# Attention and GELU feed-forward on one core: q and k of a head pair transposed together in four array quadrants, and layer 2 of the first chunk taken by quarters of its weights

## The chip, the cores and the metric

The kernel runs on one core of a Trainium2 chip. The core has five engines that run their own instruction streams and wait for each other by semaphores: TensorE (PE in the profile, with its weight loads as PEld), VectorE (DVE), ScalarE (ACT), GpSimd (POOL) and SyncE (SP). PE writes its results to PSUM, eight banks of which are shared out by hand here; DVE and ACT empty them into SBUF. DMAs are issued from POOL (loads) and SP (stores, and the transposing DMAs described below).

The metric is the device time of one execution in microseconds, as the median of several runs. Times in the profile are from one profiled execution, counted from its first instruction.

## The reference

What is computed, cut to what matters (8 batches, 8 heads, 576 tokens, 64 values per head; 4,608 tokens in all):

```python
scores = scale * q @ k.T                       # per batch and head, scale = 1/8
cum    = cumsum(max(s, 0))                     # over the tokens
bias   = -(cum[i] - cum[j])                    # added as min(bias, 0)
attn   = softmax(where(causal, scores + bias)) # over j
x      = attn @ v                              # as [4608, 512]: heads side by side
h      = x @ w_in                              # [4608, 2048]
g      = 0.5 * h * (1 + erf(h / sqrt(2)))      # exact GELU
out    = g @ w_out                             # [4608, 512]
```

## The kernel before, in words

**Two tilings that run against each other.** Attention goes by batches of 576 tokens, four pairs of heads (`p` = 0 to 3) each. The feed-forward part goes by nine chunks `c` of 512 tokens. In chunk `c` the kernel does layer 1 (`l1_item`, L487) for the 512 tokens, and then layer 2 (`l2_item`, L513) mixed with the attention of batch `c + 1`, whose result `xT` is what layer 1 of the next chunk reads. Layer 2 of a chunk is four blocks of 128 tokens (`sub`), each a sum over 16 slices of `w_out` (`ft`); an `l2_item` does the slices from `f0` to `f1` with two matmuls of 512 columns each (two column halves of the array), and after the last slice a DVE copy to `o_sb` (L530) and a store follow.

**Attention of one batch.** The steps for a pair `p` are: q and k stand transposed in `qkT`; `sc_item` (L370) makes the scores with ten matmuls and two exponentials on ACT (L394), and DVE applies the causal mask (L403, L408); `av_item` (L464) multiplies with v (`num`) and with the weights of the bias (`den`), 16 matmuls, and `norm` (L429) divides: logarithm and exponential on ACT (L433, L434), and a product on DVE (L449) that writes `xT`. v is scaled on DVE first (L230, called by `scale_pair`). The last 64 tokens of a batch are handled by `av_rest` and `norm_rest` for all pairs at once.

**How q and k get transposed.** From batch 2 on they go through DRAM: DVE interleaves two heads (L178), SP writes rows and reads them back with transposing DMAs (L194). Batches 0 and 1 come too early for that and are transposed on PE by `tr_item` (L353). `load_pair` (batch 0, one pair) and `load_early` (batch 1, two pairs) put q into one tile `early_q` and k into another, `early_k`: partitions 0 to 63 hold pairs 0 and 1, partitions 64 to 127 pairs 2 and 3. A partition holds nine consecutive tokens of a head. So one `tr_item` is 18 transposes of 64x64 (nine tokens `r`, two heads `e`) out of one row half of the array, the two heads going to the two column halves; then one copy (L364, DVE, for the very first on ACT) to `qkT`.

**PSUM.** Tag `sc` has two tiles of two banks (scores, layer 1, and `avw`), `av` three tiles of one bank, `mlp` one. The `av` tiles serve the transposes (`tr_ps`), the products with v (`avn`, `avd`), the rest tile `avr`, and those layer 2 sums that are called with `av=True`; other layer 2 sums are in `mlp`. A new tile of a tag takes a bank whose last reader is done, and PE waits for that reader.

**What sets the order.** The scheduling is by hand: each engine runs its instructions in the order in which the program names them. The start (L575 to L623) works through batch 0, with warm-up matmuls (`keep_busy`) between; L625 begins the loop over chunks, and L649 to L695 is the special mix of chunk 0 with batch 1. POOL's loads are issued in program order too, and later ones are held by small copies to `pace` (L643, L692, L721) until some result is there. The four loads of `w_out` (L611, slices 0-3, 4-7, 8-11, 12-15) are issued between the two halves of batch 1's q and k.

Of the kernel before, what the change touches and what calls it, by code (L numbers as in the profile page):

```python
# [19 lines left out]
def kernel(  # L20
# [10 lines left out]
    nc = tc.nc  # L31
    fp32 = mybir.dt.float32
    bf16 = mybir.dt.bfloat16
# [5 lines left out]
    B, H, S, D = q.shape  # L39
# [53 lines left out]
    G = 9  # L93
    early = {}

    def load_early(b, n, p):
        src = q if n == "q" else k
        if p == 0:
            early[b, n] = work.tile([128, 2, 2, G * D], bf16, tag=f"raw{n}", bufs=3, name=f"early_{n}")
        e0 = (p // 2) * 64  # L100
        nc.gpsimd.dma_start(
            out=early[b, n][e0 : e0 + 64].rearrange("g j e f -> g (j e) f"),
            in_=bass.AP(
                tensor=src.tensor,
                offset=src.offset + (b * H + 2 * p) * S * D,
                ap=[[G * D, 64], [S * D, 4], [1, G * D]],
            ),
        )

    def load_pair(b, n, p):  # L110
        src = q if n == "q" else k
        if p == 0:
            early[b, n] = work.tile([128, 2, 2, G * D], bf16, tag=f"raw{n}", bufs=3, name=f"early_{n}")
        e0 = (p // 2) * 64
        nc.gpsimd.dma_start(
            out=early[b, n][e0 : e0 + 64, p % 2],
            in_=bass.AP(
                tensor=src.tensor,
                offset=src.offset + (b * H + 2 * p) * S * D,
                ap=[[G * D, 64], [S * D, 2], [1, G * D]],  # L120
            ),
        )
# [227 lines left out]
        nc.vector.tensor_copy(bad, n)  # L350


    def tr_item(b, p, i, copy=None):  # L353
        t_ps = ps.tile([128, G, 64], bf16, tag="av", bufs=3, name="tr_ps")
        e0 = (p // 2) * 64
        src = early[b, "qk"[i]]
        for r in range(G):
            for e in range(2):
                nc.tensor.transpose(  # L359
                    t_ps[e * 64 : e * 64 + 64, r, :],  # L360
                    src[e0 : e0 + 64, p % 2, e, r * D : (r + 1) * D],
                    ident_bf[e0 : e0 + 64, e0 : e0 + 64],
                )
        (copy or nc.vector.tensor_copy)(  # L364
            qkT[b % 2][:, i, p, :S].rearrange("d (g r) -> d g r", r=G), t_ps.rearrange("d r g -> d g r")
        )

    P_of = {}

# [94 lines left out]
    def av_item(b, p, wide=False, rest=True):  # L464
        num, den = av_banks(wide)
        av_mm(b, p, num, MAIN, False)
        av_mm(b, p, den, MAIN, True)
        if rest:
            av_rest(b, p)
        norm(b, p, p + 1, num, den, 0, CUT, [(0, 0, 256), (1, 256, CUT)])  # L470
# [91 lines left out]
    def scale_pair(b, p):  # L562
        scale_v(b, ((0, ST - 1), (ST - 1, ST)), nc.vector, 2 * p, 2 * p + 2)
# [7 lines left out]
    def keep_busy(n):  # L571
        for _ in range(n):
            nc.tensor.matmul(warm, lhsT=busy[:, :128], rhs=busy, start=True, stop=True)  # L573

    weights_scan()  # L575
    keep_busy(8)
    tr_item(0, 0, 0, nc.scalar.copy)
    keep_busy(1)
    tr_item(0, 0, 1)
    keep_busy(1)  # L580
    tr_item(0, 1, 0)
    keep_busy(1)
    sc_item(0, 0, masks=False)
    nc.vector.tensor_scalar(neg_bf, tri_bf, 2048.0, -2048.0, op0=MULT, op1=ALU.add)
    tr_item(0, 1, 1)
    weights_dve()
    keep_busy(2)
    sc_item(0, 1, neg=True, units=(0,))
    tr_item(0, 2, 0)
    sc_item(0, 1, neg=True, units=(1,))  # L590
    weights_pe()
    tr_item(0, 2, 1)
    mask_item(0, 0, 0, nc.vector)
    tr_item(0, 3, 0)
    sc_item(0, 2, neg=True)
    tr_item(0, 3, 1)
    mask_item(0, 0, 1, nc.vector)
    keep_busy(1)
    sc_item(0, 3, neg=True)
# [25 lines left out]
    for c in range(NCH):  # L625
        nb = c + 1
        for k0, k1 in ((0, 2), (2, 3)) if c == 0 else ((0, 3),):
            l1_item(c, 0, k0, k1)
            l1_item(c, 1, k0, k1)
        l1_item(c, 0, KO - 1)  # L630
        l1_item(c, 1, KO - 1)
        l1_item(c, 2, av=True)
        if 0 < c and nb < B:
            scale_v(nb, STS, nc.vector)
            absmax_v(nb)
        if c == 0:
# [12 lines left out]
        if c == 0:  # L649
            exp_set()  # L650
            load_v(2)
            for p in range(NP):
                av_rest(0, p)
            tr_item(1, 0, 0)
            tr_item(1, 0, 1)
            l2_item(c, 0, 0, 8)
            tr_item(1, 1, 0)
            tr_item(1, 1, 1)
            norm_rest(0)
            sc_item(1, 0)  # L660
            l2_item(c, 1, 0, 8, av=True)
            sc_item(1, 1)
            l2_item(c, 0, 8)
            tr_item(1, 2, 0)
            tr_item(1, 2, 1)
            l2_item(c, 1, 8, av=True)
            tr_item(1, 3, 0)
            tr_item(1, 3, 1)
            scale_pair(1, 0)
            sc_item(1, 2)  # L670
            l2_item(c, 2, 0, 8, av=True)
            scale_pair(1, 1)
            sc_item(1, 3)
            l2_item(c, 2, 8, av=True)
            scale_pair(1, 2)
            av_item(1, 0, rest=False)
            scale_pair(1, 3)
            av_item(1, 1, wide=True, rest=False)
            l2_item(c, 3, 0, 8)
            interleave(2, "q")  # L680
            write_rows(2, 0, nc.sync)
            av_item(1, 2, wide=True, rest=False)
            l2_item(c, 3, 8)
            interleave(2, "k")
            write_rows(2, 1, nc.sync)
            av_item(1, 3, rest=False)
            for p in (0, 1):
                transpose_rows(2, p)
            gelu_set()
            for p in (2, 3):  # L690
                transpose_rows(2, p)
            nc.gpsimd.tensor_copy(pace, qkT[0][:, 1, 3, 0:1])  # L692
            load_qk(3)
            load_v(3)
            absmax_v(1)  # L695
        elif nb < B:
# [196 lines left out]
```

## Time and profile before

| What | Value |
|---|---|
| median of 14 runs | 331.6 us |
| lowest and highest run | 328.98 and 336.56 us |
| the profiled execution: device time | 334.04 us |
| its span, first to last instruction | 332.3 us |
| PE busy | 319.7 us, 96% |
| ACT busy | 202.2 us, 61% |
| DVE busy | 194.0 us, 58% |
| DMA, mean over the span | 143 GB/s |
| transposes on PE (`tr_ps`), share of the chain | 1% |
| layer 1 and layer 2, share of the chain | 36% and 35% |

How to read it: a line of the chain in order of time gives the start, the length and the engine with the tile, the source line and the number of instructions. A timeline line gives start, length, engine, line, operation, `out<-in`, shapes, count, and in square brackets how long the engine stood idle before it and what ended that. In the profile the names have no buffer numbers: `o_ps` is any layer 2 sum.

### The profile page before, as it was taken

How to read it: one execution, taken by the hardware profiler on the slowest of the kernel's cores; microseconds unless marked ns; L12 is line 12 of the kernel's file. 1: busy time of each engine (PE TensorE's matmuls, PEld its weight loads, DVE VectorE, ACT ScalarE, POOL GpSimd, SP SyncE). 2: the span in 40 equal slices, each digit the busy share in tenths (PEclk: the TensorE clock that was granted, in tenths of full speed). 3: DMA queues.
4: the chain of work that ended last, by engine and by line, in shares of the span. 5: the costliest groups of instructions: out<-in, count | busy, mean ns of one | idle time of the engine just before them, and what ended most of it. 6: DMA issues, size and time to landing. Idle time of an engine off the chain costs nothing.

```text
span 332.3 us, 8737 instructions
## 1 busy us (share of the span) xinstructions
PE 319.7 (96%) x3754; PEld 193.9 (58%) x3754; DVE 194.0 (58%) x385; ACT 202.2 (61%) x287; POOL 65.7 (20%) x100
## 2 busy tenths in 40 slices
PE   8879999999999999997999999999999999999993
PEld 4456666656666556654565566656665666555552
DVE  5659269996569365945477457945693664140021
ACT  3785757769576857675575777586768676204500
POOL 8754243005200740700026001400000000000000
PEclk9998999999999999999899999999999999999999
DMA  8999999845984899999869965725410010010012
GB/s 128 219 211 200 206 190 270 251 91 94 238 250 107 149 253 275 153 158 150 271 130 193 240 193 104 174 77 172 117 51 32 35 64 2 34 63 35 1 65 71
DMA packets 53837, 47.45 MB, mean 143 GB/s; under 512 B 31328, under 2 KB 43872, under 8 KB 53792
## 3 DMA queue, kind: packets, MB, share of 16 engines
q0 software_dynamic: 15936, 23.07, 39.3%
q1 hardware_dynamic: 37856, 23.75, 27.6%
q8 instruction: 31, 0.51, 0.6%
q14 instruction: 14, 0.11, 0.1%
HBM read 36.85 MB, written 16.52 MB: 161 GB/s over the span
## 4 chain that ended last, share of the span: by engine, by line
PE 90%; DMA 5%; ACT 2%; DVE 1%; issue 0%; SPq 0%
PE h_ps L501 36%; PE o_ps L523 35%; PE sc_ps L378 5%; DMA qkT<-rows 5%; PE avn L416 4%; PE avd L416 3%; PE tr_ps L359 1%; PE warm L573 1%; PE avr L416 1%; ACT P L394 1%; PE o_ps L544 1%; DVE qkT L364 1%; PE avw L416 1%; PE sc_ps L386 0%; ACT ln L434 0%; ACT ln L433 0%
## 5 line engine op out<-in xcount | busy, mean ns | idle before, releaser
L523 PE MATMUL o_ps<-w_out_r,gT 128*64 128x512 bf16 x1120 | 131.1, 383 | 0.1
L501 PE MATMUL h_ps<-xT,w_in_r 128*64 128x512 bf16 x1152 | 127.8, 383 | 1.9 <-DVE xT L449 1.9
L501 PEld LDWEIGHTS <-w_in_r 128*64 128x64 bf16 x1152 | 75.8, 111 | 51.9 <-issue 3.8
L523 PEld LDWEIGHTS <-gT 128*64 128x64 bf16 x1120 | 62.5, 111 | 49.8 <-issue 1.6
L508 ACT ACTIVATE gT<-h_ps 128x1024 bf16<-128x1024 f32 x54 | 54.3, 1022 | 50.6 <-PE h_ps L501 50.6
L394 ACT ACTIVATE P<-sc_ps 128x1024 bf16<-128x1024 f32 x64 | 62.1, 1020 | 36.5 <-PE sc_ps L378 34.3
L530 DVE COPY o_sb<-o_ps 128x512 f32<-128x512 f32 x35 | 24.0, 687 | 47.6 <-PE o_ps L523 47.5
L403 DVE TENSOR_TENSOR P<-P,tri_bf 128x512 bf16<-128x512 bf16 x58 | 24.1, 422 | 39.6 <-ACT P L394 39.4
L213 DVE TENSOR_REDUCE amx<-qkT 128x2 f32<-128x1152 bf16 x32 | 40.9, 1335 | 0.0
L202 POOL DMA_DIRECT2D raw_v<-in_v_dram x40 | 34.3, 885 | 10.7 <-DMA w_out_r<-in_moe_w_out_dram 4.2
L449 DVE SCALAR_TENSOR_TENSOR xT<-avn,ln 128x256 bf16<-128x256 f32 (+3 forms) x64 | 21.7, 385 | 24.2 <-ACT ln L434 24.1
L230 DVE TENSOR_TENSOR vv<-raw_v,wb 128x512 bf16<-128x512 f32 (+3 forms) x44 | 25.2, 632 | 0.0
L433 ACT ACTIVATE ln<-avd 128x256 f32<-128x256 f32 x56 | 18.6, 392 | 10.9 <-PE avd L416 10.9
L434 ACT ACTIVATE ln<-ln 128x512 f32<-128x512 f32 (+1 forms) x40 | 23.5, 587 | 1.3
L378 PE MATMUL sc_ps<-qkT 64*128 64x256 bf16 (+2 forms) x320 | 20.9, 250 | 3.3 <-DMA qkT<-rows 1.9
L511 ACT ACTIVATE gT<-h_ps 128x512 bf16<-128x512 f32 x36 | 19.6, 603 | 6.3 <-PE h_ps L501 6.3
L220 DVE TENSOR_REDUCE amv<-raw_v 128x1 f32<-128x2048 f32 (+1 forms) x16 | 22.9, 1470 | 0.0
L378 PEld LDWEIGHTS <-qkT 64*128 64x128 bf16 x320 | 12.9, 94 | 17.1 <-issue 10.3
L416 PEld LDWEIGHTS <-vv 128*64 128x64 bf16 x384 | 18.0, 110 | 4.1
L416 PEld LDWEIGHTS <-wb 128*64 128x64 bf16 x384 | 17.6, 112 | 0.6 <-issue 0.5
L364 DVE COPY qkT<-tr_ps 128x576 bf16<-128x576 bf16 x15 | 10.9, 753 | 10.2 <-PE tr_ps L359 10.2
L416 PE MATMUL avd<-P,wb 128*64 128x256 bf16 x224 | 15.8, 263 | 0.0
(94 smaller groups left out, 165.0 us busy)
## 6 DMA issues: line engine op xcount, KB each, us to landing
out_dram<-o_sb SPq DMA_DIRECT2D x35, 256.0 KB, 3.0
raw_v<-in_v_dram POOLq DMA_DIRECT2D x32, 256.0 KB, 8.7
rows<-qk_bf SPq DMA_DIRECT2D x12, 576.0 KB, 6.3
early_q<-in_q_dram POOLq DMA_DIRECT2D x14, 288.0 KB, 11.2
early_k<-in_k_dram POOLq DMA_DIRECT2D x14, 288.0 KB, 12.3
w_in_r<-in_moe_w_in_dram POOLq DMA_DIRECT2D x4, 512.0 KB, 10.8
w_out_r<-in_moe_w_out_dram POOLq DMA_DIRECT2D x4, 512.0 KB, 15.4
raw_v<-in_v_dram POOLq DMA_DIRECT2D x8, 128.0 KB, 10.2
```

What stands on the lines that cost most here:

```text
L202: nc.gpsimd.dma_start(out=t[:n_st, st, :, :], in_=bass.AP(tensor=v.tensor, offset=v.offset + b * H * S * D + st * 128 * D, ap=[[D, n_st], ...
L213: nc.vector.tensor_reduce(amx[:, b * NP + p], qkT[b % 2][:, :, p, :S], axis=AX, op=ALU.max, apply_absolute_value=True)
L230: eng.tensor_tensor(vb[:n_st, st0:st1, h0:h1, :], t[:n_st, st0:st1, h0:h1, :], wb[:n_st, st0:st1, b * H + h0 : b * H + h1] .unsqueeze(3).t ...
L378: nc.tensor.matmul(s_ps[:, e, off : off + n], lhsT=qkT[b % 2][e * 64 : e * 64 + 64, 1, p, jt * 128 : jt * 128 + 128], rhs=qkT[b % 2][e * 6 ...
L394: nc.scalar.activation(P[:, :, UO[u] : UO[u] + UW[u]], s_ps[:, :, : UW[u]], func=AF.Exp, scale=scale)
L403: eng.tensor_tensor(d, d, tri_bf.unsqueeze(1).unsqueeze(1).to_broadcast([128, 2, 2, 128]), op=MULT)
L416: nc.tensor.matmul(out[e * 64 : e * 64 + 64, lo : lo + n], lhsT=(wb[:, jt, b * H + h : b * H + h + 1].to_broadcast([128, 64]) if den else ...
L434: nc.scalar.activation(ln[:, :w], ln[:, :w], func=AF.Exp, scale=-1.0)
L501: nc.tensor.matmul(h_of[c, f2][i][e * 64 : e * 64 + 64], lhsT=w_in_r[:, ko, ft * 128 + e * 64 : ft * 128 + e * 64 + 64], rhs=xT[:, ko, c * ...
L508: nc.scalar.activation(gT_of[c][:, f2 * 2 : f2 * 2 + 2, :], hh_of[c, f2], func=AF.Gelu)
L523: nc.tensor.matmul(o_ps[e * 64 : e * 64 + 64], lhsT=gT[:, ft, t0 : t0 + 64], rhs=w_out_r[:, ft, :], start=(ft == 0), stop=(ft == FT - 1), ...
L530: nc.vector.tensor_copy(o_sb, o_ps)
```

## The change

It has three parts.

1. **Tiles.** For batches 0 and 1, q and k of a pair now lie in the same tile: q in partitions 0 to 63, k in 64 to 127. There is a tile for pairs 0 and 1 and one for pairs 2 and 3 (tags `rawqk0`, `rawqk1`, three buffers each), besides those of the later batches. The loads and their order stay.
2. **Transposes.** `tr_items` takes q and k of a pair together: in each of nine rounds it issues two transposes of q (upper row half) and two of k (lower row half) into two `av` tiles, and then copies both. In the start it does so for pairs 0 and 1 of batch 0, with the warm-up matmuls put together around them; pairs 2 and 3 of batch 0 are still taken q and k apart. For batch 1 all four pairs are taken together.
3. **Order in chunk 0.** Layer 2 of chunk 0 goes by quarters (four slices, 8 matmuls) for blocks 0, 1 and 3, block 2 moves ahead of the transposes of pairs 2 and 3 and into an `av` tile, and the scores, products and scalings of batch 1 stand at other places between these pieces.

The diff, cut to its core:

```diff
+    def early_tile(b, n, p):
+        key = "qk"[p // 2] if b < 2 else n
+        if (b, key) not in early:
+            early[b, key] = work.tile([128, 2, 2, G * D], bf16, tag=f"raw{key}", bufs=3, name=f"early_{key}")
+        return early[b, key], (int(n == "k") if b < 2 else p // 2) * 64
...
-    def tr_item(b, p, i, copy=None):
-        t_ps = ps.tile([128, G, 64], bf16, tag="av", bufs=3, name="tr_ps")
-        e0 = (p // 2) * 64
-        src = early[b, "qk"[i]]
+    def tr_items(b, p, its, copies=None):
+        src = early[b, "qk"[p // 2]]
+        t_ps = {i: ps.tile([128, G, 64], bf16, tag="av", bufs=3, name="tr_ps") for i in its}
         for r in range(G):
-            for e in range(2):
-                nc.tensor.transpose(
...
+            for i in its:
+                e0 = i * 64
+                for e in range(2):
+                    nc.tensor.transpose(
+                        t_ps[i][e * 64 : e * 64 + 64, r, :],
+                        src[e0 : e0 + 64, p % 2, e, r * D : (r + 1) * D],
+                        ident_bf[e0 : e0 + 64, e0 : e0 + 64],
+                    )
+        for i in its:
+            (copies[i] if copies else nc.vector.tensor_copy)(
+                qkT[b % 2][:, i, p, :S].rearrange("d (g r) -> d g r", r=G),
+                t_ps[i].rearrange("d r g -> d g r"),
+            )
...
     weights_scan()
-    keep_busy(8)
-    tr_item(0, 0, 0, nc.scalar.copy)
-    keep_busy(1)
-    tr_item(0, 0, 1)
-    keep_busy(1)
-    tr_item(0, 1, 0)
-    keep_busy(1)
+    keep_busy(9)
+    tr_items(0, 0, (0, 1), (nc.scalar.copy, nc.vector.tensor_copy))
+    keep_busy(2)
     sc_item(0, 0, masks=False)
     nc.vector.tensor_scalar(neg_bf, tri_bf, 2048.0, -2048.0, op0=MULT, op1=ALU.add)
-    tr_item(0, 1, 1)
+    tr_items(0, 1, (0, 1))
...
             for p in range(NP):
                 av_rest(0, p)
-            tr_item(1, 0, 0)
-            tr_item(1, 0, 1)
-            l2_item(c, 0, 0, 8)
-            tr_item(1, 1, 0)
-            tr_item(1, 1, 1)
+            tr_items(1, 0, (0, 1))
+            l2_item(c, 0, 0, 4)
+            tr_items(1, 1, (0, 1))
             norm_rest(0)
+            l2_item(c, 1, 0, 4, av=True)
             sc_item(1, 0)
-            l2_item(c, 1, 0, 8, av=True)
+            l2_item(c, 0, 4, 8)
+            l2_item(c, 1, 4, 8, av=True)
             sc_item(1, 1)
-            l2_item(c, 0, 8)
-            tr_item(1, 2, 0)
-            tr_item(1, 2, 1)
-            l2_item(c, 1, 8, av=True)
-            tr_item(1, 3, 0)
-            tr_item(1, 3, 1)
+            l2_item(c, 0, 8, 12)
+            l2_item(c, 1, 8, 12, av=True)
+            l2_item(c, 2, 0, 12, av=True)
+            l2_item(c, 0, 12)
+            l2_item(c, 1, 12, av=True)
+            tr_items(1, 2, (0, 1))
+            l2_item(c, 2, 12, av=True)
+            tr_items(1, 3, (0, 1))
             scale_pair(1, 0)
+            l2_item(c, 3, 0, 4)
             sc_item(1, 2)
-            l2_item(c, 2, 0, 8, av=True)
             scale_pair(1, 1)
+            l2_item(c, 3, 4, 8)
             sc_item(1, 3)
-            l2_item(c, 2, 8, av=True)
             scale_pair(1, 2)
             av_item(1, 0, rest=False)
             scale_pair(1, 3)
+            l2_item(c, 3, 8, 12)
             av_item(1, 1, wide=True, rest=False)
-            l2_item(c, 3, 0, 8)
             interleave(2, "q")
             write_rows(2, 0, nc.sync)
             av_item(1, 2, wide=True, rest=False)
-            l2_item(c, 3, 8)
+            l2_item(c, 3, 12)
             interleave(2, "k")
             write_rows(2, 1, nc.sync)
             av_item(1, 3, rest=False)
```

`load_early` and `load_pair` call `early_tile` for their destination; nothing else in them changes.

More of the change, by code (lines that the diff above doesn't have):

```diff
@@ L94 @@
     early = {}
+    def early_tile(b, n, p):
[3 more added lines that the diff above has]
+        return early[b, key], (int(n == "k") if b < 2 else p // 2) * 64
     def load_early(b, n, p):
         src = q if n == "q" else k
-        if p == 0:
-            early[b, n] = work.tile([128, 2, 2, G * D], bf16, tag=f"raw{n}", bufs=3, name=f"early_{n}")
-        e0 = (p // 2) * 64
+        t, e0 = early_tile(b, n, p)
         nc.gpsimd.dma_start(
-            out=early[b, n][e0 : e0 + 64].rearrange("g j e f -> g (j e) f"),
+            out=t[e0 : e0 + 64].rearrange("g j e f -> g (j e) f"),
             in_=bass.AP(
@@ L111, in load_pair @@
         src = q if n == "q" else k
-        if p == 0:
-            early[b, n] = work.tile([128, 2, 2, G * D], bf16, tag=f"raw{n}", bufs=3, name=f"early_{n}")
-        e0 = (p // 2) * 64
+        t, e0 = early_tile(b, n, p)
         nc.gpsimd.dma_start(
-            out=early[b, n][e0 : e0 + 64, p % 2],
+            out=t[e0 : e0 + 64, p % 2],
             in_=bass.AP(
@@ L350, in cert_4 @@
         nc.vector.tensor_copy(bad, n)
-    def tr_item(b, p, i, copy=None):
-        t_ps = ps.tile([128, G, 64], bf16, tag="av", bufs=3, name="tr_ps")
-        e0 = (p // 2) * 64
-        src = early[b, "qk"[i]]
+    def tr_items(b, p, its, copies=None):
+        src = early[b, "qk"[p // 2]]
+        t_ps = {i: ps.tile([128, G, 64], bf16, tag="av", bufs=3, name="tr_ps") for i in its}
         for r in range(G):
-            for e in range(2):
[L359 to L366, printed above, removed]
+            for i in its:
[11 more added lines that the diff above has]
+            )
     P_of = {}
@@ L588 @@
     sc_item(0, 1, neg=True, units=(0,))
-    tr_item(0, 2, 0)
+    tr_items(0, 2, (0,))
     sc_item(0, 1, neg=True, units=(1,))
     weights_pe()
-    tr_item(0, 2, 1)
+    tr_items(0, 2, (1,))
     mask_item(0, 0, 0, nc.vector)
-    tr_item(0, 3, 0)
+    tr_items(0, 3, (0,))
     sc_item(0, 2, neg=True)
-    tr_item(0, 3, 1)
+    tr_items(0, 3, (1,))
     mask_item(0, 0, 1, nc.vector)
```

## The prediction

> **What bounds the kernel now.** I read the page's chain of work first, then the chain in order of time over the stretch that the change rewrites (38 to 62 us), then the timelines of DVE and ACT there, and last the table of stretches with the granted clock.
>
> ```profile
> PE 90%; DMA 5%; ACT 2%; DVE 1%; issue 0%; SPq 0%
> ```
>
> ```profile
> 9.38 0.39 PE sc_ps L378 x4
> ...
> 39.06 0.69 PE tr_ps L359 x36
> 39.75 1.85 PE o_ps L523 x16
> 41.60 0.69 PE tr_ps L359 x36
> 42.28 0.55 PE sc_ps L378 x10
> ...
> 49.69 0.69 PE tr_ps L359 x36
> 50.38 0.55 PE sc_ps L378 x10
> 50.92 1.85 PE o_ps L523 x16
> 52.77 0.55 PE sc_ps L378 x10
> 53.32 1.85 PE o_ps L523 x16
> ```
>
> The columns are start, length, what. The reader should see that between 39 and 62 us the chain never leaves PE: each piece starts where the last ended. PE is the bound there, and time taken off it is won only if no wait appears. The cover is also visible: after each q and k pair of transposes (36 in 0.69) come 16 layer 2 matmuls (1.85).
>
> ```profile
> 8.56 0.76 DVE L364 COPY qkT<-tr_ps 128x576 bf16<-128x576 bf16 x1
> ...
> 39.51 1.42 DVE L364 COPY qkT<-tr_ps 128x576 bf16<-128x576 bf16 x2 [5.65 <-PE tr_ps L359]
> ...
> 59.47 0.81 DVE L178 COPY qk_bf<-early_q 128x1152 bf16<-128x1152 bf16 x2
> 60.59 0.76 DVE L449 SCALAR_TENSOR_TENSOR xT<-avw,ln 128x256 bf16<-128x256 f32 x2 [0.31 <-ACT ln L434]
> ```
>
> ```profile
> 50.74 1.94 ACT L394 ACTIVATE P<-sc_ps 128x1024 bf16<-128x1024 f32 x2 [3.67 <-PE sc_ps L378]
> 53.14 1.94 ACT L394 ACTIVATE P<-sc_ps 128x1024 bf16<-128x1024 f32 x2 [0.45 <-PE sc_ps L378]
> 55.97 0.66 ACT L433 ACTIVATE ln<-avd 128x256 f32<-128x256 f32 x2 [0.90 <-PE avd L416]
> 56.66 0.63 ACT L434 ACTIVATE ln<-ln 128x512 f32<-128x512 f32 x1
> ```
>
> DVE needs 1.42 us to empty the two transpose tiles of a pair; ACT needs 1.94 for the exponentials of a pair and about 1.3 for one normalisation.
>
> ```profile
> 20.00:23.40 3.40, 1.55 (x25) 0.99 (x21) 1.51 (x4) 3.31 (x10) 2.09 (x3) 1.00 1.24 205
> 23.40:26.80 3.40, 3.40 (x20) 1.93 (x18) 2.87 (x5) 2.50 (x5) 1.04 (x2) 0.50 1.27 216
> 153.10:156.50 3.40, 1.50 (x26) 0.95 (x24) 1.43 (x3) 0.66 (x1) 0.00 (x0) 1.00 1.63 192
> 156.50:160.00 3.50, 3.50 (x32) 1.88 (x28) 1.74 (x5) 2.47 (x5) 0.00 (x0) 0.51 0.94 188
> ```
>
> The first time of a row is the stretch's length, the second PE busy; the figure before the last two is the granted clock. A stretch with PE busy for 1.5 of 3.4 us was followed by one at half clock, twice.
>
> **What the Trainium skill says.** "TensorEngine Tiling (Array Packing)", PSUM Bottleneck: tiling speeds up the array and not the emptying of PSUM, so the copy may become the limit. The trace agrees: 0.69 against 1.42 us. "TensorE: Matmul & The Clock Gate", Part 3: matmuls in different row groups overlap. The score rows agree: the ten matmuls stream 1,024 columns per row half; at the 0.108 us per 512-column matmul of the o_ps row (1.73 for 16, two side by side) that is 0.43 us side by side and 0.86 in turn, and the chain has 0.55 with the change of array shape. Part 1 there: idle PE brings half clock, as in the last view. "Perfetto Trace Analysis", Optimization Strategy: a repeating gap on the saturated engine can mean too few PSUM buffers. Before shows none; the change asks for two tiles at once from the pool "av" of three.
>
> **The change, part by part.** Times are on the clock of the profiled execution. Handovers from its trace: a copy starts 0.24 after the last transpose of its tile starts (39.27 to 39.51), PE starts 0.06 after a copy ends (8.56+0.76 to 9.38), changing the array's shape costs PE 0.1.
>
> *Transposes of batch 1.* q's 18 take 38.99 to 39.30, nine rounds of two in 0.31. With q and k in the two row halves I take nine rounds of four in the same 0.31, so 0.41 instead of 0.69: four times 0.28 saves 1.13. Bounds: nothing (halves in turn) to 1.13.
>
> *Pool waits.* "av" holds the rest tile avr until norm_rest; the built order gives each wait.
> (a) Pair 1's k tile takes the bank of pair 0's k. Pair 0's last transpose starts at 39.30, its copies end 40.26 and 40.97, so k may start at 41.03. PE has only one quarter of layer 2 (8 matmuls, 0.86) in between and is ready at 40.38: idle 0.65. Before had 1.85 there. Behind the waiting transpose on PE stand the other 33 of its group, then o_1 and the scores of pair 0; DVE's next copies wait for it too.
> (b) Layer 2's second token block (o_1), now right behind, takes pair 1's q bank: last transpose 41.31, copy to 42.26, start 42.32, ready 41.4: idle 0.95. Behind it on PE stand the scores of pair 0, for which ACT's exponentials wait. Before had those scores (0.55) in between and started o_1 0.02 after they ended.
> (c) Pair 2's k tile takes o_1's bank just after o_1's last matmul: 0.38 for that matmul, 0.05, copy 0.69 (o_sb rows), 0.06 make 1.18; PE is there after 0.31: idle 0.87. Before gave pair 2 no bank that had only just been filled.
> (d) Pair 3 again has 8 matmuls of cover, as in (a): idle 0.65. Behind it stand layer 2 of the fourth block and the scores of pair 2, on which the tail below depends.
> Only if a copy could free its bank halfway would these shrink; the trace has no such case, so I price them whole and let the low end take half.
>
> *The tail.* Layer 2 of the third token block moves ahead of the transposes, so from the scores of pair 2 to layer 1 of chunk 1 PE has about 7.3 us of work instead of 11.2 (50.31 to 61.52). ACT has two exponential pairs (3.9) and the norms in that stretch. Counted from the scores of pair 2: their second PSUM tile is free at 0.43+1.94+0.06=2.43, PE wants it at 1.70 (scores 0.55, a quarter 0.86, the next scores' first tile 0.22, shape changes): idle 0.73. Exponentials end at 4.34; DVE masks pair 3 (0.42+0.22) and only then scales v of pair 2 (about 0.66), so its product starts at 5.7, not 5.2: idle 0.52. ACT then does three norms of 1.3 and ends the third at 8.27; DVE has just begun the interleave of q (0.87) and needs 0.76 for the product after it, so xT of pair 2 is there at 9.9, and layer 1 waits 1.36 in all. Check: 9.9 less 7.3 is 2.6, and 0.73+0.52+1.36 = 2.61. In before the third norm was ready (61.35) before layer 1 began (61.52).
>
> *w_out by quarters.* The four loads are issued at 19.8 to 23.7 and take 12.7 to 17.7 to land, so all is there by 41.4, and before first used the last quarter near 46. No wait to remove: nothing.
>
> *Start.* Scores of pair 0 come 0.45 earlier, but pair 1's q and k are transposed together after them. k is issued at 3.15 and takes 4.8 to land: 7.95. First round then, last transpose 8.22, copies (1.48 in a row) from 8.46 to 9.9: the scores of pair 1 start at 9.95 instead of 9.38, and all up to layer 1 stands behind them on PE. Cost 0.5; at least 0.4, since the row then only waits longer for what it already waited for, at most 0.6. That pair 0's scores are earlier is worth nothing, as ACT then waits for those of pair 1. The 14 warm-up matmuls are as many as before and hide beside the loads; neg_bf (0.60 on DVE) moves into the wait for k.
>
> *Nothing:* POOL and SP issue the same transfers in the same order, into other tiles; the new tile tags take SBUF only. ACT's order is unchanged.
>
> **Sum.** 0.65+0.95+0.87+0.65+2.61 = 5.73, less 1.13, plus 0.5: +5.1 us. What follows is unchanged and starts on PE's progress (the load pacing at L643 waits for gT 70.3 us in all), so it shifts rigidly. The profiled execution (span 332.3, device time 334.04) would become 339.1. It lies 2.4 above the median of 331.6; I add the same 5.1 to the median: **336.7 us**, 1.5% slower.
>
> **Rivals.**
> Row halves in turn: no saving, and each copy pair starts later; +6.5, 338.1. For it: no row here shows four quadrants. Against: the scores.
> Clock: (a) and (b) put 1.6 us of idling into some 2 us, (c) and (d) 1.5 into 2.5, close to the 1.85 that halved the clock before. One stretch of 3.4 at half clock costs up to 1.7: 338.4, two 340.1.
> Absorbed, not slower by more than can be told: at 153.5 to 155.4 PE waited 1.90 for transposed rows and then lost 1.75 to half clock. If those transfers kept their own time, a later PE would meet them ready: 5.1-3.65 = +1.45, 333.05. It decides once the rows come at least 1.9 us less late than PE. Against: their loads and rows are issued on PE's progress.
> The waits don't appear, because copies end inside 0.86 us of cover: 331.6+0.5-1.13 = 331.0. It would need copies of about 0.35 instead of 0.71.
>
> **How the numbers follow.** Forecast 0.57, halves in turn 0.15, clock 0.20, absorbed 0.03, no waits 0.03; 0.02 is left for a gain that no case here gives. A measurement of this kernel tells about 0.5% (1.7 us) from no change. So slower is 0.92 (the first three), same 0.06 (absorbed and no waits both lie inside 1.7 us), faster 0.02. The range begins 2.5 below the forecast (334.2), where somewhat less than half of the 5.73 of waits doesn't come, and ends at two stretches of half clock (336.7 plus 3.4, and 0.3 for the start and the copies: 340.4).
>
> **What would show it.** Right: PE idle before tr_ps and o_ps by DVE between 40 and 57 us, four times 0.6 to 1.0; PE idle before h_ps by DVE xT near 66; 36 transposes in some 0.4; scores of pair 1 near 9.95; layer 1 of chunk 1 under way 5 us later. Wrong: a PE chain without holes there, or transposes still at 0.69. The forecast fails if DVE's copies overlap the next round, or if the later DMA waits shrink as PE falls back.

## The result, and the profile after

The changed kernel takes 342.44 us (median of 10 runs, 336.93 to 350.03); the kernel before took 334.37 beside it (median of 47 runs, 328.49 to 346.36). The ratio is 1.0265, 95% interval 1.0210 to 1.0319: about 8.8 us slower, where 5.1 were forecast. The ratios, here and below, leave slow, disturbed executions of either kernel out, so they aren't the quotients of the medians. The direction was right and the size was not: 342.44 lies outside the range of 334.2 to 340.4.

The profiled execution of after takes 337.92 us, only 3.9 more than that of before. That is because the profiled execution of before carried delays that after's did not: 1.65 us of half clock in chunk 0, and 1.90 us of waiting with 1.7 of half clock behind it in chunk 3. That 337.92 lies near the 339.1 that the prediction gave for this execution is therefore chance.

| part, us (on PE, from its first layer 1 matmul to the next chunk's) | before | after | after minus before | less before's own delays |
|---|---|---|---|---|
| start, to layer 1 of chunk 0 | 21.97 | 22.26 | +0.29 | +0.29 |
| chunk 0 | 39.55 | 40.88 | +1.33 | +2.98 |
| chunk 1, layer 1 | 13.81 | 14.68 | +0.87 | +0.87 |
| chunk 1, the rest | 20.83 | 21.77 | +0.94 | +0.94 |
| chunk 2 | 34.05 | 38.07 | +4.02 | +4.02 |
| chunk 3 | 37.68 | 34.05 | -3.63 | 0 |
| chunks 4 to 8, to the last matmul | 158.57 | 158.57 | 0 | 0 |

The last column sums to 9.1, close to the 8.8 of the ratio and to the 8.4 between the lowest runs (336.93 and 328.49). (The 1.65 is the difference of layer 1 of chunk 0 in the two, 16.40 and 14.75. Experiment 9 confirms it: there the same PE instructions of chunk 0 took 37.90 at full clock.) The first three rows are what the prediction priced: 4.1 us together. The two rows after them, 5.0 us, it priced at nothing.

The wait of before in chunk 3 is this line of its PE timeline:

```profile
155.41 0.61 PE L378 MATMUL sc_ps<-qkT 64*128 64x256 bf16 x10 [1.90 <-DMA qkT<-rows]
```

The page's line of shares of after, and the table of stretches with the granted clock, at the places where before was shown:

```profile
PE 70%; DMA 17%; POOL 4%; DVE 3%; ACT 2%; issue 2%; SPq 0%; DVEq 0%; POOLq 0%
```

```profile
20.00:23.40 3.40, 1.55 (x28) 1.07 (x24) 1.51 (x4) 3.30 (x9) 2.57 (x4) 1.00 1.24 204
23.40:26.80 3.40, 3.40 (x32) 2.18 (x33) 2.57 (x5) 3.15 (x6) 0.74 (x1) 1.00 1.26 218
...
38.00:42.00 4.00, 2.76 (x70) 1.42 (x57) 3.18 (x5) 2.41 (x4) 1.17 (x2) 1.00 1.20 233
```

PE held 90% of the chain before and holds 70% now; DMA went from 5 to 17%. Most of that DMA share misleads. The chain in order of time has these loads:

```profile
12.73 14.02 DMA w_in_r<-in_moe_w_in_dram
...
27.80 15.37 DMA early_k<-in_k_dram
...
43.46 8.42 DMA early_q<-in_q_dram
```

They are 37.8 us, or 11% of the span, and are in the chain only because the last of them landed just as a wait of PE ended (at 51.90, see below). The other 5%, 18.0 us, lie in chunks 1 and 2, and they matter. The clock is not the reason in this execution: it is full (1.00, the figure before the last two) also between 38 and 42 us, where PE works only 2.76 of 4.00.

PE's timeline of after in chunk 0 (start, length, instruction; in brackets the idle time before it and what ended that):

```profile
39.03 0.22 PE L362 MATMUL tr_ps<-ident_bf,early_q 64*64 64x64 bf16 x2
39.64 0.47 PE L362 MATMUL tr_ps<-ident_bf,early_q 64*64 64x64 bf16 x34 [0.40 <-DVE qkT L368]
40.95 1.05 PE L528 MATMUL o_ps<-w_out_r,gT 128*64 128x512 bf16 x8 [0.85 <-DVE qkT L368]
...
51.90 0.47 PE L362 MATMUL tr_ps<-ident_bf,early_k 64*64 64x64 bf16 x34 [0.64 <-DMA early_q<-in_q_dram]
...
53.88 0.47 PE L362 MATMUL tr_ps<-ident_bf,early_k 64*64 64x64 bf16 x34 [0.38 <-DVE qkT L368]
...
57.69 0.40 PE L383 MATMUL sc_ps<-qkT 64*128 64x256 bf16 x6 [0.50 <-ACT P L399]
...
64.44 1.92 PE L506 MATMUL h_ps<-xT,w_in_r 128*64 128x512 bf16 x16 [0.68 <-DVE xT L454]
```

The predicted waits are there, all but that for v (0.12 us, too short to be marked). The one at 51.90 names a DMA, but that is chance: a load happened to land then. DVE's timeline shows the real releaser, the emptying of o_1's bank, which the waiting tile takes over:

```profile
51.15 0.69 DVE L535 COPY o_sb<-o_ps 128x512 f32<-128x512 f32 x1 [0.17 <-PE o_ps L528]
52.40 1.42 DVE L368 COPY qkT<-tr_ps 128x576 bf16<-128x576 bf16 x2 [0.56 <-PE tr_ps L362]
```

Here the copy ends at 51.84 and the transposes go on at 51.90; the next copies cannot begin before 52.40. In experiment 8 the same wait of 0.6 us is put down to `o_sb`.

ACT's timeline in the tail of chunk 0, where the four exponentials of pairs 2 and 3 and then the norms follow each other:

```profile
55.70 3.77 ACT L399 ACTIVATE P<-sc_ps 128x1024 bf16<-128x1024 f32 x4 [8.99 <-PE sc_ps L383]
59.33 0.69 ACT L438 ACTIVATE ln<-avd 128x256 f32<-128x256 f32 x2
60.05 0.63 ACT L439 ACTIVATE ln<-ln 128x512 f32<-128x512 f32 x1
60.64 0.66 ACT L438 ACTIVATE ln<-avw 128x256 f32<-128x256 f32 x2
```

ACT has no marked idle time from 55.70 until the third norm is done (63.17), after 8.99 us in which it had nothing to do: its work now comes together at the end.

What the prediction did not have is in chunk 2. PE's timeline there, and DVE's:

```profile
122.83 0.61 PE L383 MATMUL sc_ps<-qkT 64*128 64x256 bf16 x10
126.64 0.60 PE L421 MATMUL avn<-P,vv 128*64 128x256 bf16 x8 [3.20 <-DVE P L408]
127.68 0.52 PE L421 MATMUL avd<-P,wb 128*64 128x256 bf16 x6 [0.45 <-DVE xT L454]
```

```profile
118.48 0.68 DVE L535 COPY o_sb<-o_ps 128x512 f32<-128x512 f32 x1
125.19 0.97 DVE L180 COPY qk_bf<-early_q 128x1152 bf16<-128x1152 bf16 x2 [6.02 <-DMA early_q<-in_q_dram]
126.08 0.74 DVE L408 TENSOR_TENSOR P<-P,tri_bf 128x512 bf16<-128x512 bf16 x2
```

PE waits 3.20 us for a mask of 0.4 us. The mask is late because in DVE's program order the interleave of batch 4's q stands ahead of it, and DVE waits 6.02 us for that load to land. In before the same wait was 1.93 us, and PE waited for nothing:

```profile
117.66 0.97 DVE L178 COPY qk_bf<-early_q 128x1152 bf16<-128x1152 bf16 x2 [1.93 <-DMA early_q<-in_q_dram]
118.56 0.74 DVE L403 TENSOR_TENSOR P<-P,tri_bf 128x512 bf16<-128x512 bf16 x2
```

The chain in order of time says why the load is late:

```profile
112.40 3.76 DMA qkT<-rows
116.15 0.02 issue
116.18 0.04 POOLq L724
...
118.07 6.93 DMA early_q<-in_q_dram
```

POOL holds batch 4's loads, by the copy to `pace` (L724), until the last transposing DMA of batch 3 has landed. That DMA is a link of a loop: rows written, rows transposed, `pace`, next batch's loads, interleave, next rows.

### The profile page after: what moved, and what is told of

Same layout as the page of the kernel before. It is cut to its first block, busy times and chain, and to the rows that moved or that the text cites. A ratio compares the mean times of both kernels' runs of the same rounds, so it can differ in the third digit from the quotient of the medians.

```text
span 336.1 us, 8738 instructions
## 1 busy us (share of the span) xinstructions
PE 316.4 (94%) x3754; PEld 193.1 (57%) x3754; DVE 193.2 (57%) x385; ACT 202.2 (60%) x287; POOL 65.7 (20%) x100
## 4 chain that ended last, share of the span: by engine, by line
PE 70%; DMA 17%; POOL 4%; DVE 3%; ACT 2%; issue 2%; SPq 0%; DVEq 0%; POOLq 0%
PE h_ps L506 32%; PE o_ps L528 27%; DMA early_q<-in_q_dram 7%; DMA early_k<-in_k_dram 5%; DMA w_in_r<-in_moe_w_in_dram 4%; PE sc_ps L383 3%; PE avn L421 3%; PE avd L421 3%; ACT P L399 2%; DMA qkT<-rows 1%; DVE xT L454 1%; POOL raw_v L204 1%; PE o_ps L549 1%; PE avr L421 1%; POOL early_q L117 1%
## 5 line engine op out<-in xcount | busy, mean ns | idle before, releaser
L506 PE MATMUL h_ps<-xT,w_in_r 128*64 128x512 bf16 x1152 | 126.4, 379 | 2.5 <-DVE xT L454 2.5
L506 PEld LDWEIGHTS <-w_in_r 128*64 128x64 bf16 x1152 | 76.6, 110 | 50.4 <-issue 3.3
L421 PE MATMUL avn<-P,vv 128*64 128x256 bf16 x224 | 15.8, 263 | 3.3 <-DVE P L408 3.2
```

Source lines behind the costliest of these rows:

```text
L421: nc.tensor.matmul(out[e * 64 : e * 64 + 64, lo : lo + n], lhsT=(wb[:, jt, b * H + h : b * H + h + 1].to_broadcast([128, 64]) if den else ...
L506: nc.tensor.matmul(h_of[c, f2][i][e * 64 : e * 64 + 64], lhsT=w_in_r[:, ko, ft * 128 + e * 64 : ft * 128 + e * 64 + 64], rhs=xT[:, ko, c * ...
```

## The experiments

Theory A is the prediction's: chunk 0 pays its own waits, and everything later shifts rigidly. Theory B: chunk 0 also puts the loop of rows and loads late against PE, and PE pays for that in chunks 1 to 3. The kernel before had medians of 335.64 beside experiments 1 to 4, 337.09 beside 5, 6, 7 and 10, 334.85 beside 8 and the repeats of 3 and 7, and 334.62 beside 9. For 5, 6, 7 and 10 there is no ratio: what they show has to come from the trace.

**1. The order of chunk 0 undone** (the start, the tiles and the quadrants stay):

```diff
             tr_items(1, 0, (0, 1))
-            l2_item(c, 0, 0, 4)
+            l2_item(c, 0, 0, 8)
...
-            l2_item(c, 2, 0, 12, av=True)
-            l2_item(c, 0, 12)
-            l2_item(c, 1, 12, av=True)
             tr_items(1, 2, (0, 1))
-            l2_item(c, 2, 12, av=True)
+            l2_item(c, 1, 8, av=True)
             tr_items(1, 3, (0, 1))
```

> The changed kernel with the pieces of chunk 0 in the order of before (16 matmuls of layer 2 between transposes); tiles, quadrants and start as changed. If the waits of the new order are what the time went into, PE idles in chunk 0 for about 1.1 us only (0.5 before the second layer 2 block, 0.6 before pair 3's k), layer 1 of chunk 1 starts within 0.5 us of before's place, and no wait of DVE on early_q stops PE in chunk 2: ratio to before 0.995 to 1.005. If instead the merged tiles or the four quadrants themselves cost time, or the new start, it stays at 1.01 or more.

337.99 us (335.63 to 339.77), ratio 1.0163 [1.0048, 1.0278]: by the number, the expectation failed. But its runs had a clock of 0.970 to 0.987, and the profiled one spent 13.7 us of its start at half clock and reached chunk 0 at 27.36 instead of 22.26. So the time says little, and the trace more: no wait of PE in chunks 1 to 3, against 1.34 and 3.64 us in chunks 1 and 2 of after. The later waits come with the new order of chunk 0, not with the tiles, the quadrants or the start, which this kernel keeps.

**2. Batch 4's loads issued early**, right behind `load_v(3)` in chunk 0, without their `pace`:

```diff
             load_v(3)
+            load_qk(4)
...
-                        nc.gpsimd.tensor_copy(pace, qkT[(nb + 1) % 2][:, 1, p, 0:1])
-                        load_qk(nb + 2)
```

> The changed kernel, with the loads of batch 4's q and k issued right after those of batch 3 instead of after the last transposing DMA of batch 3. Theory A (rigid shift: everything after chunk 0 moves as a block, the rest is the clock): no difference from the changed kernel, ratio 1.02 to 1.03. Theory B (the chain of transposing DMAs, loads, interleave and rows falls 4 us behind PE and stops DVE, then PE, in chunk 2): the wait of PE before avn for DVE (3.2 us) and of DVE for early_q (6.0 us) are gone, and the ratio falls by 0.008 to 0.013, to about 1.015.

345.48 us, ratio 1.0414 [1.0306, 1.0522]: not the 1.015 of theory B, and rather slower than the changed kernel (the intervals just touch). The wait for the mask in chunk 2 is gone, but in chunk 2 PE now waits for transposed rows:

```profile
114.76 1.06 PE L528 MATMUL o_ps<-w_out_r,gT 128*64 128x512 bf16 x8
123.22 1.03 PE L383 MATMUL sc_ps<-qkT 64*128 64x256 bf16 x10 [7.40 <-DMA qkT<-rows]
```

The transposing DMAs of batch 3 were in flight from 104.2 to 130.6 us and took up to 17.2 us each, against 4.6 at most in after. Beside them ran the loads of batch 4 (until 112.9), and also those of v and of batch 5 (from 105.9 on), which stood behind the removed `pace` and so came earlier too. That these loads delayed the transposing DMAs is likely from the times, and not shown apart. "The load is late" is only the visible end of the loop, and pulling that end did not help.

**3. Quadrants alone**: `tr_items(1, p, (0, 1))` for batch 1, with order and start of before.

```diff
-            tr_item(1, 0, 0)
-            tr_item(1, 0, 1)
+            tr_items(1, 0, (0, 1))
             l2_item(c, 0, 0, 8)
```

> Only tiles and quadrants of the change in batch 1: chunk 0 and the start in the order of before. By my walk of the built order the saving of 1.13 us is taken back by two new waits (0.5 before the second layer 2 block, 0.6 before pair 3's k), so layer 1 of chunk 1 starts 0.3 us earlier than before: ratio 0.997 to 1.001. Against e1 it gives the price of the new start: 0.3 to 0.6 us. If quadrants brought their whole 1.13 us, ratio 0.996.

332.68 us, ratio 0.9969 [0.9834, 1.0104]. Once more, with more runs:

> Quadrants for batch 1 alone, order and start of the kernel before, once more for a narrower interval (0.9969 [0.9834, 1.0104] in three rounds). Quadrants worth their duration less the wait for o_ps: 4 times 0.28 less 0.3 to 0.6, so 0.5 to 0.8 us under the kernel before, ratio 0.9976 to 0.9985; a gain that a measurement can hardly tell.

333.75 us (median of 23, 328.68 to 339.88), ratio 0.9977 [0.9927, 1.0027]. The saving on PE is there in the trace (36 transposes in 0.41 us), less one wait of 0.32 for a bank (and in this execution a stop of 1.72 us, see the last section); in time it cannot be told from nothing.

**4. The kernel before with a bare delay**: 24 idle matmuls (5.2 us) ahead of the scores of pair 2 in chunk 0.

```diff
+            delay = ps.tile([128, 512], fp32, tag="mlp", bufs=1, name="delay")
+            for _ in range(24):
+                nc.tensor.matmul(delay, lhsT=busy[:, :128], rhs=busy, start=True, stop=True)
             sc_item(1, 2)
```

> The kernel before with 24 idle matmuls (5.2 us on PE) put ahead of the scores of pair 2 in chunk 0. Theory A (rigid): 5.2 us longer, ratio 1.0155, and no new wait in chunk 2. Theory B in its strong form (any delay in chunk 0 makes the transfers fall behind PE): ratio 1.025, with DVE waiting some 6 us for early_q and PE some 3 us in chunk 2. Theory B in its weak form (only the order of the change, in which rows are written late against PE, does that): as A.

341.17 us, ratio 1.0149 [0.9987, 1.0311], too wide to tell the theories apart; the trace does. PE's wait in chunk 2 is 0.80 us, not 3.6. Shifting PE and everything behind it together does not make the loop late; in this A is right. It takes a delay of the rows against PE.

**5. The changed kernel once more.**

> The changed kernel once more, beside the three that follow. Theory A (the waits of chunk 0 are the whole cost, the rest shifts rigidly): ratio to the kernel before near 1.0155, and no wait over 1 us on PE in chunk 2. Theory B (DVE's wait for batch 4's q in chunk 2 holds the masks back and is part of what the change costs): ratio near 1.0265, and PE idle 2 to 4 us ahead of an avn in chunk 2 again, released by DVE's P L408.

344.67 us (340.0 to 346.18), beside 337.09 for the kernel before. Chunk 0 repeats to the hundredth (0.40, 0.85, 0.64, 0.38, 0.50 us). The later waits come again, in other places:

```profile
126.28 0.60 PE L421 MATMUL avn<-P,vv 128*64 128x256 bf16 x8 [1.65 <-DVE P L408]
...
165.89 1.03 PE L383 MATMUL sc_ps<-qkT 64*128 64x256 bf16 x10 [5.30 <-DMA qkT<-rows]
```

So A is out. The second line is the wait that before's profile had with 1.90 us, now 5.30: the same loop, met one step further on. With it came half clock (163.3 to 170.1 us), which made chunk 3 another 2.0 us longer (41.38 in all, against 34.05 in after).

**6. DVE's queue in chunk 2 turned round**: masks of pair 1 first, then the interleave.

```diff
-                if nb + 1 < B and p == 1 + late:
+                if nb + 1 < B and p == 1 + late and c != 2:
                     interleave(nb + 1, "q")
                     write_rows(nb + 1, 0, nc.sync)
...
                 av_item(nb, p - 1)
+                if nb + 1 < B and p == 1 + late and c == 2:
+                    interleave(nb + 1, "q")
+                    write_rows(nb + 1, 0, nc.sync)
```

> The changed kernel, but in chunk 2 alone the interleave of batch 4's q stands on DVE behind the masks of pair 1 and the product of pair 0, instead of ahead of them; chunk 0 is that of the changed kernel. Theory B: the 3.2 us wait of PE in chunk 2 goes or falls under 0.8 us, time 2.5 to 3.5 us under the changed kernel of this job. Theory A: no difference to the changed kernel. A third outcome (C): the wait comes back a chunk later, before the scores of batch 4 (rows later by about 1 us), and the time stays.

341.55 us (338.96 to 345.54), against 344.67 for the changed kernel beside it; the ranges overlap. The third outcome came: the wait for the mask is gone, and others are there.

```profile
129.76 2.56 PE L528 MATMUL o_ps<-w_out_r,gT 128*64 128x512 bf16 x22 [1.84 <-DVE o_sb L535]
...
161.86 0.61 PE L383 MATMUL sc_ps<-qkT 64*128 64x256 bf16 x10 [4.43 <-DMA qkT<-rows]
```

**7. The tail of chunk 0 undone, and nothing else.** Layer 2 of the third block goes back around the scores of pairs 2 and 3, and the fourth block to halves; the transposes keep their quadrants and the short cover, but (c) has no cause any more.

```diff
-            l2_item(c, 2, 0, 12, av=True)
             l2_item(c, 0, 12)
-            l2_item(c, 1, 12, av=True)
             tr_items(1, 2, (0, 1))
-            l2_item(c, 2, 12, av=True)
+            l2_item(c, 1, 12, av=True)
             tr_items(1, 3, (0, 1))
...
             sc_item(1, 2)
+            l2_item(c, 2, 0, 8, av=True)
...
             sc_item(1, 3)
+            l2_item(c, 2, 8, av=True)
```

> The changed kernel with only the end of chunk 0 put back: layer 2 of the third token block stands around the scores of pairs 2 and 3 again, as in the kernel before, the transposes keep their quadrants and the quarters' cover of 8 matmuls. Theory A: the waits of the tail go (scores of pair 3, v of pair 2, xT: measured about 1.7 us), and nothing else: 1.5 to 2.5 us under the changed kernel. Theory B in its strong form (the tail is what throws batch 2's rows and the loads behind them late against PE): also the wait in chunk 2 goes, 4.5 to 6 us under the changed kernel.

330.67 us (330.29, 330.60, 330.75 and one run of 337.24), with the changed kernel at 344.67 (340.0 at the lowest) and the kernel before at 337.09 (328.96 at the lowest) in the same series. The strong form of B holds: PE idles 0.03 us in chunk 1 and not at all in 2 and 3, though waits (a) and (b) are as in after (0.39 and 0.85), with 0.45 left before pair 3. Once more:

> The changed kernel with the end of chunk 0 put back, once more (330.67 and no wait on PE after chunk 0 in the first run). If this is what it is and not that run's luck: again 330 to 331 in most runs, level with the fastest runs of the kernel before plus 1 to 2 us, and under its median where that kernel waits for batch 4's rows in chunk 3.

334.3 us (median of 22, 330.47 to 342.27), ratio 1.0037 [0.9991, 1.0083]; ten of the runs lie between 330.4 and 331.9. Again no wait in chunks 1 to 3.

**8. The tail kept, only the rows early**: this tells whether the tail works through the rows.

```diff
             scale_pair(1, 0)
+            interleave(2, "q")
+            write_rows(2, 0, nc.sync)
...
             scale_pair(1, 1)
+            interleave(2, "k")
+            write_rows(2, 1, nc.sync)
...
-            interleave(2, "q")
-            write_rows(2, 0, nc.sync)
...
-            interleave(2, "k")
-            write_rows(2, 1, nc.sync)
```

> The changed kernel with one thing moved: the interleave of batch 2's q and k and the two writes of its rows stand on DVE behind the v scalings of pairs 0 and 1 (data landed at 54.2 and 56.0 us there) instead of behind the products of the tail. The waits of chunk 0 stay, the one for v scaling in the tail may grow from nothing to about 1 us, that for xT of pair 2 shrinks by as much. If the rows of batch 2 carry the loss into chunks 2 and 3: rows written 5 to 7 us earlier against PE, batch 3's loads issued 4 to 6 us earlier, PE's waits in chunks 1 to 3 fall from 4 to 8 us to under 1.5, time 3 to 6 us under the changed kernel (its two jobs: 342.4 and 344.7). If the loss came from the tail by another way: still 342 to 345.

334.88 us (333.09 to 338.05), ratio 1.0133 [1.0013, 1.0252]. All of chunk 0's waits are still there, with the expected new one for v:

```profile
60.69 0.40 PE L383 MATMUL sc_ps<-qkT 64*128 64x256 bf16 x6 [0.50 <-ACT P L399]
...
64.23 0.57 PE L421 MATMUL avw<-P,vv 128*64 128x256 bf16 x8 [0.62 <-DVE vv L232]
```

In chunks 1 to 3 PE idles 0.15 us in all. DVE's wait in chunk 2 is short enough for the mask to come in time:

```profile
122.54 0.97 DVE L180 COPY qk_bf<-early_q 128x1152 bf16<-128x1152 bf16 x2 [1.33 <-DMA early_q<-in_q_dram]
```

What remains, 1.33% with a wide interval, is what chunk 0 costs by itself: its trace has 3.5 us more in chunk 0 than the order of before at full clock (41.40, against 37.90 in experiment 9). The forecast's 1.5% lies within that interval.

**9. The kernel before, only the rows late**: the converse.

```diff
-            interleave(2, "q")
-            write_rows(2, 0, nc.sync)
...
-            interleave(2, "k")
-            write_rows(2, 1, nc.sync)
+            interleave(2, "q")
+            write_rows(2, 0, nc.sync)
             av_item(1, 3, rest=False)
+            interleave(2, "k")
+            write_rows(2, 1, nc.sync)
```

> The kernel before, nothing of the change in it, but the interleave and row writes of batch 2 one place later each on DVE (q where k stood, k behind the products of pair 3), so that they are issued 1.2 and 3.2 us after layer 1 of chunk 1 begins on PE instead of 1.2 us before and 1.2 after; in the changed kernel it was 0.6 and 2.6 after. PE's chunk 0 is unchanged. If late rows alone are enough for the loss in chunks 1 to 3: PE idle 2 to 5 us in chunks 1 to 3, released by masks or rows, and 2 to 5 us over the kernel before (1.006 to 1.015). If the waits of chunk 0 are needed too: no difference, 0.997 to 1.003.

337.43 us (334.76 to 341.79), ratio 1.0208 [1.0093, 1.0323]; up to 1.015 was expected. PE's chunk 0 has no new wait, nothing of the change is in it, and chunk 2 looks like after's:

```profile
118.89 0.61 PE L378 MATMUL sc_ps<-qkT 64*128 64x256 bf16 x10
122.58 0.96 PE L416 MATMUL avn<-P,vv 128*64 128x256 bf16 x8 [3.08 <-DVE P L403]
```

```profile
121.14 0.97 DVE L178 COPY qk_bf<-early_q 128x1152 bf16<-128x1152 bf16 x2 [5.91 <-DMA early_q<-in_q_dram]
```

Late rows are enough. Chunks 1 and 2 take 5.6 us more than in before: 3.7 of waiting, and most of the rest from 3.4 us at half clock from the end of the wait on. All profiles side by side, times of issue counted from layer 1 of chunk 1 on PE:

| kernel | rows of batch 2 written: q, k | batch 3's loads issued | PE idle in chunks 1, 2, 3 |
|---|---|---|---|
| rows early (8) | -6.29, -3.86 | +15.5 | 0.15, 0, 0 |
| before | -1.22, +1.18 | +17.0 | 0.03, 0, 1.90 |
| tail undone (7), its repeat | -1.21, +1.18; -1.12, +1.28 | +16.8; +16.1 | 0.03, 0, 0; 0.02, 0, 0 |
| old order (1) | -1.12, +1.28 | +15.9 | 0.02, 0, 0 |
| quadrants alone (3), its repeat | -1.14, +1.26 (both) | +15.9; +16.2 | 0.03, 0, 0; 0.02, 0.15, 1.16 |
| bare delay (4) | -1.22, +1.18 | +17.5 | 0.03, 0.80, 0 |
| after, its repeat (5) | +0.62, +2.61 (both) | +20.5; +20.2 | 1.34, 3.64, 0; 1.43, 2.09, 5.30 |
| loads early (2) | +0.61, +2.61 | +20.4 | 1.41, 7.40, 0 |
| masks first (6) | +0.61, +2.61 | +20.3 | 1.22, 1.84, 4.43 |
| q and k apart (10) | +0.61, +2.61 | +20.3 | 1.22, 2.06, 1.55 |
| rows late (9) | +1.18, +3.08 | +19.5 | 0.54, 3.17, 0 |

In the rows with late writes from after's order, 0.68 us of chunk 1 is the wait for `xT`, which is the tail's own. The table splits in two: k's rows at most 1.3 us after layer 1 begins, loads at 17.5 or sooner, and 1.9 us of waiting at most; or 2.6 and later, loads from 19.5 on, and 3.7 to 8.8. Against the kernel before, k's rows are 1.4 to 1.9 us late, and the loads 2.5 to 3.5.

**10. After's order, q and k transposed apart.**

```diff
-            tr_items(1, 0, (0, 1))
+            tr_items(1, 0, (0,))
+            tr_items(1, 0, (1,))
```

> The changed kernel with its order and its tiles kept, but q and k of a pair in batch 1 transposed one after the other (two groups of 18, 0.31 us each and a change of quadrants between) instead of 36 in rounds of four. If the quadrants are worth what their duration says: PE has 4 times 0.28 = 1.1 us more of transposes, but each copy begins with the first group, so the waits for pool av shrink by 0.3 to 0.5 each: within 1 us of the changed kernel, that is, PE's saving is bought back by waits on DVE's copies. If the saving were real time, it would be 1.1 us slower than the changed kernel.

342.33 us (337.79 to 342.59), against 344.67 for the changed kernel beside it; the ranges overlap. Chunk 0 takes 40.05 us, 0.83 less than after's 40.88, with four times 0.28 more of transposes in it: of the four waits for banks only 0.44 and 0.39 are left.

```profile
40.09 0.88 PE L362 MATMUL tr_ps<-ident_bf,early_q 64*64 64x64 bf16 x36
41.42 1.05 PE L528 MATMUL o_ps<-w_out_r,gT 128*64 128x512 bf16 x8 [0.44 <-DVE qkT L368]
```

In this order the quadrants lose on PE more than they save: with two tiles asked for at once, and rounds that alternate between them, q's copy cannot begin before k's bank is free.

## Why the prediction was wrong in size

**Right.** Transposes: 36 in 0.40 us, the forecast's 0.41. All four waits for banks, at the predicted places and with the predicted releasers. The tail's waits for ACT and for `xT`. The quarters of `w_out`: no wait removed. No half clock behind (a) to (d), in any profile of this order. The scores of pair 1 at 9.67, forecast 9.95.

**Right in kind, the tail too large.** The marked idle times at (a) to (d) are 0.40, 0.85, 0.64 and 0.38, 2.27 in all; 3.12 were forecast. But idle time is counted from the modelled end of the transposes ahead of a wait: the two at 39.03 last 0.22 us there, while a whole group follows itself from start to start in 0.40. From start to start, as the prediction counted, the three held-up stretches of transposes take 1.92 (39.03 to 40.95, with (a) and (b)), 1.26 and 1.00 us where a free group takes 0.40. That is 2.98 us lost, so the prices of (a) to (d) were nearly right together. The mis-sized terms are the tail and the start. The tail's 0.73, 0.52 and 1.36 came out as 0.50, 0.12 and 0.68 of idle time, and from start to start as 1.8 for 2.61; the start as 0.29 for 0.5. Layer 2 in smaller pieces took 0.2 more, which the sum left out (eight of its matmuls between pieces of another array shape take 0.98 us, 54.28 to 55.26, not 0.86). Together: 2.98+1.8+0.29+0.2, less 1.13, is 4.1 for 5.1.

**The step that failed** is this one: "What follows is unchanged and starts on PE's progress (the load pacing at L643 waits for gT 70.3 us in all), so it shifts rigidly." The pacing that counts in chunks 1 and 2 isn't L643. The loads of batches 3 and 4 hang on the last transposing DMA of the batch ahead (L692, L721), as POOL's timeline of before says:

```profile
77.99 0.18 POOL L692 CAST pace<-qkT 128x1 f32<-128x1 bf16 x1 [23.96 <-DMA qkT<-rows]
...
109.54 0.18 POOL L721 CAST pace<-qkT 128x1 f32<-128x1 bf16 x1 [24.30 <-DMA qkT<-rows]
```

That DMA hangs on row writes which stand on DVE behind the products of the tail. The tail made these 1.4 to 1.8 us later against PE, even though PE itself waited for the tail. Priced at nothing, this cost 5.0 us in chunks 1 and 2 of the profiled execution. Experiment 8 took that delay away and left the tail: the 5.0 us went. Experiment 9 put such a delay alone into the kernel before: 2.1% came, 0.9 to 3.2 by the interval. The prediction had seen the waiting at 153.5 to 155.4 and used it only as a possible cushion ("absorbed"). It was the mark of a loop without slack, which here passed lateness on. That DVE already waited 1.93 us for batch 4's q in chunk 2 of before, with masks queued behind, was in the trace and wasn't read.

**How 1.4 us became 3.5** is shown in part. Against layer 1 of chunk 1, and compared with before, k's rows are issued 1.4 us late in after and have landed 1.9 late; the last transposing DMA of batch 2 is issued 1.9 late and has landed 3.5 late. It took 4.3 us instead of 2.6, and in all five profiles of late rows that keep the loads' place (after, its repeat, 6, 9, 10) it took 3.7 to 4.3. In each of them a 16 KiB packet of the instruction queue ran 1.1 to 2.0 us after that DMA's issue; in before (75.20 issued, packet at 77.59) and in 7 (74.91 and 77.31) it came when the DMA was nearly done. These are the two lines for 78 to 84 us of after's DMA view (queue, kind: packets, MB, share of the engines):

```profile
q1 hardware_dynamic: 1352, 0.32, 58.6%
q8 instruction: 1, 0.02, 1.5%
```

The packet is one of 1,353. That it is the cause was not tried by itself, and it can't be the only one: in experiment 8 a transposing DMA of batch 2 took 3.85 us with no such packet within 5 us. Where in chunks 1 to 3 the wait appears also differs from run to run, and that stays open.

Of the rivals: row halves in turn are out, since 36 transposes took 0.40 us. The clock took nothing where its rival had it, in chunk 0; but half clock came with the later waits in the profiles of 2, 5, 6 and 9 (3.4 to 10.2 us of it), so part of the measured 8.8 can be clock that those waits brought. "Absorbed" was the opposite of what happened.

## What to carry to other kernels

When work is repacked to keep the busiest engine busy, check what else is queued behind the pieces that move: here the costly victim was a DRAM write on DVE's and SP's queues that PE doesn't need for another 15 us. A long wait on an engine that is not the bound, in a loop of loads and writes that paces itself, can be a sign that the loop has no slack, as it was here; ask there whether a delay is passed on or enlarged, and don't take it as shifted. Don't read a share of the chain off the page before its releasers are checked: one chance landing made 11% of it. Saving 1.1 us of PE by asking for two PSUM tiles at once needs the emptying engine to keep pace; here 1.42 us of copies against 0.98 of cover took it back.

No version beat the kernel before by more than its interval: quadrants alone 0.9977 [0.9927, 1.0027], the tail undone 1.0037 [0.9991, 1.0083].

## What had not been expected of the hardware

PE can stop in mid-stream with nothing to wait for that the profile shows. This is quadrants alone (3), in the transposes of pair 2:

```profile
48.21 0.37 PE L362 MATMUL tr_ps<-ident_bf,early_k 64*64 64x64 bf16 x21
50.30 0.32 PE L362 MATMUL tr_ps<-ident_bf,early_k 64*64 64x64 bf16 x15 [1.72 <-issue]
```

In experiments 1, 3 and 4 PE stopped for 0.62, 1.72 and 3.00 us, each time after the 21st of these 36 transposes, with a packet of the instruction queue 2.7 to 3.2 us before PE went on. In the repeat of 3 it stopped there for 0.59, and 128 matmuls further on for 1.09; so it did in 1 (1.09) and in the repeat of 7 (1.30). The Trainium skill, "Runtime: NRT & Kernel Launch", section Instruction fetch mechanics, says that instructions are fetched in blocks of 16 KiB, 256 instructions, at a cost that is mostly hidden. The trace agrees with the block: a matmul has its own weight load, so 128 matmuls are 256 instructions, and the packets are of 16 KiB. That PE waited for its instructions is argued from this and not tried by itself; if it did, the cost was not hidden here, up to 3.0 us. Batch 2's loads were landing then, but so they were in before. Up to this place experiment 4 is the kernel before, whose profile has no such stop; why some executions have it stays open.
